# Reordering the vector work between two matmul stages: Sinkhorn rounds, token sums, a maximum and a scaling

## The chip, the cores and the metric

One core of a Trainium2 chip runs the whole program. The metric is device time in microseconds (us) of that core, from one launch; smaller is better. TensorE (PE in the profile, PEld for its weight loads) does the matrix products, VectorE (DVE) and ScalarE (ACT) do elementwise work, GpSimd (POOL) does elementwise work on SBUF, and SyncE (SP) issues the DMAs.

## What is computed

Three stages follow each other. The middle of the reference, cut:

```python
attn_out = _attn_ref(**attn_kwargs)             # bucketed attention, 2 x 8 heads, 768 x 64
x = attn_out.transpose(0, 2, 1, 3).reshape(1536, 512)
h = x @ w_in                                    # 512 -> 2048
x = (h * np.tanh(softplus(h))) @ w_out          # 2048 -> 512
# mixture of 8 experts, every token through every expert
logits = x @ w_gate
P = np.exp(logits - logits.max())
for _ in range(8):
    P /= P.sum(1, keepdims=True) + 1e-09        # rows: over 8 experts
    P /= P.sum(0, keepdims=True) + 1e-09        # columns: over 1536 tokens
    P *= N / E
for e in range(8):
    out += P[:, e:e + 1] * (np.maximum(x @ w1[e], 0.0) @ w2[e])
```

The eight rounds of rows and columns (Sinkhorn rounds) work on a matrix of 1536 tokens by 8 experts. It is held as `prob`, 128 partitions x 12 x 8.

## The kernel before, in words

Every float32 product is made of three matmuls on rounded parts: high by high, high by low, low by high. The low part of a matrix is the difference between it and its rounded copy. For weights ScalarE writes the high part and GpSimd the low part; for activations VectorE writes the low part.

**Attention** takes the first part of the time and is not touched.

**The MLP** runs 48 steps (`steps`, L818). A step `n` issues 12 matmuls of `up` (L831 to L833) into a PSUM bank; ScalarE applies Mish and rounds (`act`, L841, L842), and VectorE writes the rest `gl` (L843). `down(n - 3)` then adds 12 matmuls (L856) into four banks. When a group of four steps ends for a block of 512 tokens, VectorE adds the four banks into `acc` (`evacuate`, L866). Every engine executes its instructions in the order in which they were issued. A side table (`at`) issues further work at the end of a step: the gate logits of a token block (`logits`: eight matmuls at L884, transposes at L890, an addition at L891), and the sums and differences of activations that the next stage needs (`make_t`, L987 to L998). For each of two chunks `kc` there are four sums, k = 1, 2, 4, 3. Numbers 1 and 3 take four VectorE instructions, numbers 2 and 4 three; the last of them waits for a ScalarE copy.

**The expert stage** runs 64 units, each a quarter of one expert for half of the tokens. A unit's first part is seven products `s` = 0 to 6 of six matmuls (L1141), into two PSUM banks; after each, `post` lets ScalarE and VectorE read the bank. After product 1, VectorE makes the total `u` from its bank (L1161), and product 3 adds to that same bank, so it waits for this read. After product 6 VectorE writes four rests `gl` (L1154). Then 36 matmuls of `second` (L1208) follow in four runs, 0 to 3. A table of jobs (`job(u, s, ...)`) hangs further work behind product `s` of unit `u`, or, with s = 7 to 10 (`NP1` is 7), behind the runs of `second`. The slot (u, 8) carries the next weights' splitting (`unit_a_hi`, `unit_s_hi` on ScalarE; `unit_a_lo` at L1010, L1011 and `unit_s_lo` at L1027 on GpSimd) and, in units 1 to 8, one Sinkhorn round on VectorE. The job (u, -1) splits the next `w` matrix (ScalarE L1030, GpSimd L1034). Every fourth unit VectorE also takes finished output tiles out of PSUM (`gather`, L1220 to L1226).

A round is `sinkhorn_rows` (reduce L920, add L921, reciprocal L922, product L923) and `sinkhorn_cols` (reduce L926, transposes L902, reduce L903, add L928, reciprocal L929, transposes L932, product L933), each instruction on the result of the one before.

Of the kernel before, what the change touches and what calls it, by code (L numbers as in the profile page):

```python
# [12 lines left out]
AF = mybir.ActivationFunctionType  # L13
ALU = mybir.AluOpType
AX = mybir.AxisListType

P = 128
# [36 lines left out]
Q = 32  # L54
# [7 lines left out]
def lsh_attention_moe_kernel(  # L62
# [13 lines left out]
    nc = tc.nc  # L76
# [727 lines left out]
    prob = acc_p.tile([P, NTOK // P, E], F32, name="prob")  # L804
# [88 lines left out]
    def small(name, p, n=1):  # L893
        return sk_p[0].tile([p, n], F32, tag=name, name=name)

    def quarters(x):
        return [x[a * Q:(a + 1) * Q] for a in range(P // Q)]

    def across(x, op, negate=False):
        y, r = small("y", Q, P), small("r", Q)  # L900
        for a, part in enumerate(quarters(x)):
            nc.vector.transpose(out=y[:, a * Q:(a + 1) * Q], in_=part)  # L902
        nc.vector.tensor_reduce(out=r, in_=y, axis=AX.X, op=op, negate=negate)  # L903
        return r

    def sinkhorn_max():
        m = small("m", P)
        nc.vector.tensor_reduce(out=m, in_=prob, axis=AX.XY, op=ALU.max)
        r = across(m.to_broadcast([P, Q]), ALU.max, negate=True)
        m = small("nm", P)  # L910
        for part in quarters(m):
            nc.vector.tensor_copy(part, r)
        return m

    def sinkhorn_exp(r):
        nc.scalar.activation(prob, prob, AF.Exp, bias=r[:, 0:1])
# [20 lines left out]
    def tile_of(i):  # L937
        return acc[:, i // KC, i % KC, :]

    def scale_first(i):  # L940
        dst = tile_of(i)
        nc.vector.tensor_scalar(out=dst, in0=dst, scalar1=prob[:, i, 0:1], scalar2=None, op0=ALU.mult)
        nc.vector.scalar_tensor_tensor(
            out=dst, in0=tile_of(i + NT // 2), scalar=prob[:, i, 1:2], in1=dst, op0=ALU.mult, op1=ALU.add
        )
# [4 lines left out]
    def at(n, f, *args):  # L950
        side.setdefault(n, []).append(lambda: f(*args))

    box = {}

    def put(key, f, *keys):
        def g():
            box[key] = f(*[box[k] for k in keys])
        return g

    LAG = 3  # L960
    done_at = {tb: n + LAG for n, (g, tb, _) in enumerate(steps) if g == NG - 1}
    for tb in range(NTB - 1):
        at(done_at[tb] + (6 if tb else 3), logits, tb)

    tw = []

# [78 lines left out]
        parts_t(0, k, kc, a)  # L1045
        held[kc] = a

    for n, k, kc in ((1, 1, 0), (2, 2, 0), (2, 4, 0), (3, 3, 0), (3, 1, 1), (4, 2, 1), (4, 4, 1), (5, 3, 1)):
        at(done_at[1] + n, make_t, k, kc)
    free = {}  # L1050
    for n, (_, _, i) in enumerate(steps):
# [182 lines left out]
    def job(u, s, f, *args):  # L1234
        jobs.setdefault((u, s), []).append(lambda: f(*args))

    NP1 = len(PRODUCTS)
# [13 lines left out]
    for f in splits:  # L1251
        job(0, 5, f)
    job(0, NP1 + 2, logits, NTB - 1, ps_u, "u0")
    job(1, 0, put("m", sinkhorn_max))
    job(1, 2, lambda: sinkhorn_exp(box["m"]))
    for x in range(8):
        job(1 + x, NP1 + 1, sinkhorn_rows)
        job(1 + x, NP1 + 1, sinkhorn_cols)
    for i in range(NT // 2):
        job(9 + i // 3, NP1 + 1, scale_first, i)  # L1260

    half = NU // 2

# [95 lines left out]
```

## Time and profile before

| what | value |
|---|---|
| median of three runs | 1553.04 us (1551.37 to 1553.8) |
| the profiled execution's own time | 1551.87 us |
| its span, first to last instruction | 1550.0 us |
| TensorE busy, of the span | 98%, weight loads 87% |
| VectorE, ScalarE, GpSimd busy | 61%, 45%, 61% |
| share of the chain of waits by engine | PE 83%, DVE 11% |

A busy TensorE row is no measure of its speed, since matmuls overlap. What a stage costs is read from the length of a unit, and what it lost from the idle time in front of TensorE's instructions and weight loads.

### The profile page before, as it was taken

The numbers are of one execution on the slowest core, as the hardware profiler recorded it, in microseconds if no ns is written. First come the engines' busy times: TensorE is split into PE (matmuls) and PEld (weight loads), VectorE is DVE, ScalarE is ACT, GpSimd is POOL, SyncE is SP. The second block draws the span as 40 slices with busy tenths as digits, with TensorE's granted clock in tenths as the row PEclk, the third lists the DMA queues.
The fourth block names the chain that finished last, engine by engine and source line by source line (L and its number), as shares of the span: only waits on it lengthen the run. The fifth ranks groups of instructions, "written<-read, shape, count | busy, mean of one in ns | idle before, by whom it ended". The sixth has DMA issues, their size and how long they took to land.

```text
span 1550.0 us, 20648 instructions
## 1 busy us (share of the span) xinstructions
PE 1523.0 (98%) x7492; PEld 1348.1 (87%) x7492; DVE 945.6 (61%) x1546; ACT 694.1 (45%) x1266; POOL 941.2 (61%) x785
## 2 busy tenths in 40 slices
PE   8999999999999999999999999999999999999999
PEld 7898888888888887888989898999999999999998
DVE  8899995867633678787453557654535344445353
ACT  5878776654423343333333334343333333333331
POOL 6888876433313485656666666667666666666661
PEclk9999999999999999999999999999999999999999
DMA  7755540222200122121222222223222222222211
GB/s 188 164 141 139 150 118 15 82 68 82 69 27 1 41 69 69 57 66 58 70 65 70 67 69 67 69 67 110 68 69 68 69 68 69 68 69 68 69 55 41
DMA packets 65989, 117.67 MB, mean 76 GB/s; under 512 B 18320, under 2 KB 19320, under 8 KB 65888
## 3 DMA queue, kind: packets, MB, share of 16 engines
q1 hardware_dynamic: 65888, 116.36, 25.6%
q8 instruction: 59, 0.97, 0.3%
q14 instruction: 42, 0.34, 0.1%
HBM read 93.41 MB, written 3.15 MB: 62 GB/s over the span
## 4 chain that ended last, share of the span: by engine, by line
PE 83%; DVE 11%; issue 2%; POOL 1%; ACT 1%; DMA 1%; SPq 0%; DVEq 0%; ACTq 0%; POOLq 0%
PE y L1208 30%; PE u L1141 29%; PE y L856 7%; PE pav L488 4%; PE h L833 2%; PE h L832 2%; PE h L831 2%; DVE gl L1154 1%; PE pst L438 1%; PE pst L439 1%; PE ps L386 1%; DVE mx L400 1%; DVE prob L923 1%; POOL plo L450 0%; DMA vt<-in_v_dram 0%
## 5 line engine op out<-in xcount | busy, mean ns | idle before, releaser
L1149 ACT ACTIVATE gh<-c 128x384 fp32r<-128x384 f32 x256 | 134.7, 526 | 192.5 <-DVE c L1161 190.4
L1154 DVE SCALAR_TENSOR_TENSOR gl<-c,gh 128x384 fp32r<-128x384 f32 x256 | 195.5, 827 | 0.0
L1161 DVE TENSOR_TENSOR u<-u,p 128x384 f32<-128x384 f32 x64 | 35.6, 556 | 258.2 <-PE u L1141 258.2
L1208 PE MATMUL y<-ww,gh 128*128 128x512 f32 x768 | 186.6, 391 | 0.0
L1208 PE MATMUL y<-w,gh 128*128 128x512 f32 x768 | 186.0, 391 | 0.0
L1208 PEld LDWEIGHTS y<-w,gh 128*128 128x128 f32 x768 | 143.7, 188 | 28.9
L1208 PEld LDWEIGHTS y<-ww,gh 128*128 128x128 f32 x768 | 143.7, 188 | 28.8
L450 POOL TENSOR_TENSOR plo<-p,ph 128x384 fp32r<-128x384 f32 x128 | 139.9, 1105 | 30.3 <-ACT ph L447 16.8
L1034 POOL TENSOR_TENSOR w<-stage,w 128x1024 fp32r<-128x1024 f32 x32 | 76.6, 2393 | 92.0 <-ACT w L1030 92.0
L1034 POOL TENSOR_TENSOR ww<-stage,ww 128x1024 fp32r<-128x1024 f32 x32 | 76.6, 2392 | 84.2 <-ACT ww L1030 84.2
L856 PE MATMUL y<-gh,w 128*128 128x512 f32 x336 | 109.9, 389 | 0.0
L444 ACT ACTIVATE p<-pst 128x384 f32<-128x384 f32 x192 | 92.5, 486 | 38.0 <-PE pst L439 32.2
L1030 ACT CAST ww<-stage 128x1024 fp32r<-128x1024 f32 x32 | 33.6, 1049 | 162.3 <-PE y L1208 162.3
L1030 ACT CAST w<-stage 128x1024 fp32r<-128x1024 f32 x32 | 33.6, 1049 | 161.3 <-PE y L1208 161.3
L1141 PE MATMUL u<-tw,w 128*128 128x384 f32 x480 | 94.2, 342 | 9.5 <-DVE u L1161 9.5
L1010 POOL TENSOR_TENSOR wx<-stage,wx 128x512 fp32r<-128x512 f32 x32 | 44.9, 1403 | 96.1 <-ACT wx L1005 91.2
L148 POOL TENSOR_TENSOR stage<-stage,sgn 128x512 f32<-128x512 f32 x32 | 43.0, 1345 | 99.1 <-DVE sgn L146 93.6
L400 DVE TENSOR_REDUCE mx<-ps 128x1 f32<-128x768 f32 x95 | 90.0, 948 | 15.1 <-PE ps L386 14.3
L1010 POOL TENSOR_TENSOR wa<-stage,wa 128x512 fp32r<-128x512 f32 x32 | 45.6, 1424 | 87.8 <-ACT wa L1005 87.8
L1208 PE MATMUL y<-ww,gl 128*128 128x512 f32 x384 | 98.2, 389 | 0.0
L1208 PE MATMUL y<-w,gl 128*128 128x512 f32 x384 | 97.4, 389 | 0.0
L1141 PE MATMUL u<-tw,ws 128*128 128x384 f32 x480 | 92.1, 337 | 4.2 <-DVE u L1161 4.1
(232 smaller groups left out, 3996.6 us busy)
## 6 DMA issues: line engine op xcount, KB each, us to landing
stage<-in_w_dram SPq DMA_DIRECT2D x160, 512.0 KB
raw<-in_qk_dram SPq DMA_DIRECT2D x13, 384.0 KB
wx<-hi SPq DMA_DIRECT2D x20, 192.0 KB
vt<-in_v_dram SPq DMA_DIRECT2D x16, 192.0 KB
out_dram<-acc SPq DMA_DIRECT2D x11, 256.0 KB
zq<-hi SPq DMA_DIRECT2D x11, 192.0 KB
ak<-hi SPq DMA_DIRECT2D x11, 192.0 KB
zq<-lo SPq DMA_DIRECT2D x11, 192.0 KB
```

What stands on the lines that cost most here:

```text
L400: nc.vector.tensor_reduce(out=m[:, t, 0:1], in_=s_t[t][:, :, :HALF], axis=AX.XY, op=ALU.max, negate=True)
L444: nc.scalar.activation(p_t[u, c], st_t.pop((u, c))[:, :HALF], AF.Exp, scale=0.125)
L450: (nc.gpsimd if e == "P" else nc.vector).tensor_sub(out, in0, in1)
L488: nc.tensor.matmul(av_t[u][:, :HALF], x.rearrange("p a d -> p (a d)"), y, start=False, stop=(c == NKC - 1 and n == len(pairs) - 1),)
L856: nc.tensor.matmul(yps[j], x, y, start=(head and m == 0), stop=(tail and m == 2))
L1010: nc.gpsimd.tensor_sub(a[:, 1, 0:512], t[:, 0, :], f32(a)[:, 0, 0:512])
L1030: nc.scalar.copy(wbuf[u % 2]["w"][:, 0, :], staged["u", u, 1].rearrange("p c n -> p (c n)"))
L1034: nc.gpsimd.tensor_sub(y[:, 1, :], t, f32(y)[:, 0, :])
L1141: nc.tensor.matmul(bank[x], weight(u, a, m, kc), moving(u, b, mm, kc), start=(first and n == 0), stop=(n == 5), skip_group_check=not first)
L1149: nc.scalar.activation(hi, src, AF.Relu)
L1154: nc.vector.scalar_tensor_tensor(out=lo, in0=src, scalar=0.0, in1=f32(hid_u[u, c][0]), op0=ALU.max, op1=ALU.subtract)
L1208: nc.tensor.matmul(y_t[t], (hi, hi, lo)[m][:, t % 3 * P:(t % 3 + 1) * P], y, start=(k == 0 and first), stop=(k == NF // 2 - 1 and last),)
```

## The change

```diff
     def sinkhorn_max():
         m = small("m", P)
         nc.vector.tensor_reduce(out=m, in_=prob, axis=AX.XY, op=ALU.max)
-        r = across(m.to_broadcast([P, Q]), ALU.max, negate=True)
+        return across(m.to_broadcast([P, Q]), ALU.max, negate=True)
+
+    def sinkhorn_spread(r):
         m = small("nm", P)
...
     def scale_first(i):
         dst = tile_of(i)
-        nc.vector.tensor_scalar(out=dst, in0=dst, scalar1=prob[:, i, 0:1], scalar2=None, op0=ALU.mult)
+        nc.scalar.activation(dst, dst, AF.Copy, scale=prob[:, i, 0:1])
...
-        at(done_at[tb] + (6 if tb else 3), logits, tb)
+        at(done_at[tb] + 3, logits, tb)
...
-    for n, k, kc in ((1, 1, 0), (2, 2, 0), (2, 4, 0), (3, 3, 0), (3, 1, 1), (4, 2, 1), (4, 4, 1), (5, 3, 1)):
+    for n, k, kc in ((1, 1, 0), (1, 2, 0), (2, 4, 0), (2, 3, 0), (3, 1, 1), (3, 2, 1), (4, 4, 1), (4, 3, 1)):
         at(done_at[1] + n, make_t, k, kc)
...
-    job(1, 0, put("m", sinkhorn_max))
-    job(1, 2, lambda: sinkhorn_exp(box["m"]))
+    job(1, 1, put("r", sinkhorn_max))
+    job(1, 3, put("m", sinkhorn_spread, "r"))
+    job(1, NP1, lambda: sinkhorn_exp(box["m"]))
     for x in range(8):
         job(1 + x, NP1 + 1, sinkhorn_rows)
-        job(1 + x, NP1 + 1, sinkhorn_cols)
+        job(2 + x, NP1 + 1, sinkhorn_cols)
     for i in range(NT // 2):
-        job(9 + i // 3, NP1 + 1, scale_first, i)
+        job(10 + i // 3, NP1 + 1, scale_first, i)
```

`done_at[1]` is step 42. The sums of steps 43 to 47 now stand in steps 43 to 46, two in each, and the logits of the second token block are issued in step 45 instead of step 48. Unit 1 does the rows of the first round alone, units 2 to 8 the columns of a round and the rows of the next, and unit 9 the last columns. The scaling of the first tiles follows in units 10 and 11.

**VectorE in the slot of a Sinkhorn round.** Before, the first rows behind a unit's rests, up to the total of the next unit:

```order
L920 TENSOR_REDUCE rsum<-prob 128x12
L921 TENSOR_SCALAR rsum<-rsum 128x12
L922 RECIPROCAL rsum<-rsum 128x12
L923 TENSOR_TENSOR prob<-prob,rsum 128x96
L926 TENSOR_REDUCE csum<-prob 128x8
L902 STREAM_TRANSPOSE y<-csum 32x32 x4
L903 TENSOR_REDUCE r<-y 32x1
L928 TENSOR_SCALAR r<-r 32x1
L929 RECIPROCAL r<-r 32x1
L932 STREAM_TRANSPOSE i<-r 32x32 x4
L933 SCALAR_TENSOR_TENSOR prob<-i,prob 128x96
L1161 TENSOR_TENSOR u<-u,p_6284 128x384
```

The same slot of units 2 to 8 now (the lines behind the edit are two higher):

```order
L928 TENSOR_REDUCE csum<-prob 128x8
L902 STREAM_TRANSPOSE y<-csum 32x32 x4
L903 TENSOR_REDUCE r<-y 32x1
L930 TENSOR_SCALAR r<-r 32x1
L931 RECIPROCAL r<-r 32x1
L934 STREAM_TRANSPOSE i<-r 32x32 x4
L935 SCALAR_TENSOR_TENSOR prob<-i,prob 128x96
L922 TENSOR_REDUCE rsum<-prob 128x12
L923 TENSOR_SCALAR rsum<-rsum 128x12
L924 RECIPROCAL rsum<-rsum 128x12
L925 TENSOR_TENSOR prob<-prob,rsum 128x96
L1163 TENSOR_TENSOR u<-u,p_6268 128x384
```

The same eleven rows stand in front of the total, with the seven of the columns ahead of the four of the rows.

**VectorE at the end of the MLP.** Before, from the rest of step 46 (`t` and `tw` are the sums of the next stage, `lgs` the logits):

```order
L843 TENSOR_TENSOR gl<-t,gh 128x512
L992 TENSOR_TENSOR t<-xh,xl 128x384
L993 TENSOR_TENSOR t<-t 128x384
L998 TENSOR_TENSOR tw<-t,tw 128x384
L992 TENSOR_TENSOR t<-xh,xl 128x384
L993 TENSOR_TENSOR t<-t 128x384
L998 TENSOR_TENSOR tw<-t,tw 128x384
L843 TENSOR_TENSOR gl<-t,gh 128x512
L987 TENSOR_TENSOR t<-xh 128x384
L988 TENSOR_TENSOR t<-xl 128x384
L989 TENSOR_TENSOR t<-t 128x384
L998 TENSOR_TENSOR tw<-t,tw 128x384
```

Now, from the same rest:

```order
L843 TENSOR_TENSOR gl<-t,gh 128x512
L994 TENSOR_TENSOR t<-xh,xl 128x384
L995 TENSOR_TENSOR t<-t 128x384
L1000 TENSOR_TENSOR tw<-t,tw 128x384
L989 TENSOR_TENSOR t<-xh 128x384
L990 TENSOR_TENSOR t<-xl 128x384
L991 TENSOR_TENSOR t<-t 128x384
L1000 TENSOR_TENSOR tw<-t,tw 128x384
L843 TENSOR_TENSOR gl<-t,gh 128x512
L866 TENSOR_TENSOR acc<-y_5711,acc 128x512
L866 TENSOR_TENSOR acc<-y_5715,acc 128x512
L866 TENSOR_TENSOR acc<-y_5719,acc 128x512
```

The last sum of four instructions stood behind the rest of step 47 (the second `gl`) and stands ahead of it now; the logits' transposes, which followed that sum, have moved up behind the rest of step 45.

## Rows read from the trace of the kernel before

**Rows 1.** Waits of TensorE's weight loads from 255 us on: total, times, longest us

```profile
PEld u L1141 <- DVE u L1161: 16.9, 10, 3.1
```

**Rows 2.** Stretches of units 0, 1, 3, 4, 8, 10: busy time by engine, PEclk, DMA

```profile
530.41:551.43 21.02, 19.22 (x88) 16.45 (x87) 13.96 (x24) 9.71 (x18) 16.77 (x14) 0.92 0.09 25
551.43:567.35 15.92, 15.78 (x79) 14.02 (x78) 12.63 (x27) 7.54 (x12) 13.90 (x11) 1.00 0.44 133
...
584.19:601.02 16.83, 15.80 (x80) 14.04 (x78) 13.53 (x27) 5.88 (x10) 9.97 (x8) 1.00 0.20 63
601.02:619.65 18.63, 15.81 (x80) 14.04 (x79) 16.89 (x33) 5.88 (x10) 9.94 (x8) 1.00 0.18 58
...
670.15:690.36 20.21, 17.39 (x80) 15.63 (x78) 17.02 (x33) 5.88 (x10) 9.94 (x8) 0.92 0.17 53
...
707.18:722.72 15.54, 15.54 (x80) 14.09 (x78) 11.70 (x16) 5.89 (x10) 10.28 (x8) 1.00 0.23 69
```

**Rows 3.** VectorE in order of time, units 1 and 2: start, us, line, idle before

```profile
553.62 0.62 DVE L912 COPY nm<-r 32x1 f32<-32x1 f32 x4
...
579.63 0.24 DVE L920 TENSOR_REDUCE rsum<-prob 128x12 f32<-128x96 f32 x1
579.91 0.43 DVE L921 TENSOR_SCALAR rsum<-rsum 128x12 f32<-128x12 f32 x1
...
580.63 2.13 DVE L923 TENSOR_TENSOR prob<-prob,rsum 128x96 f32<-128x96 f32 x1
582.80 0.33 DVE L926 TENSOR_REDUCE csum<-prob 128x8 f32<-128x96 f32 x1
...
584.35 0.14 DVE L928 TENSOR_SCALAR r<-r 32x1 f32<-32x1 f32 x1
...
585.60 2.40 DVE L933 SCALAR_TENSOR_TENSOR prob<-i,prob 128x96 f32<-128x96 f32 x1
587.92 0.55 DVE L1161 TENSOR_TENSOR u<-u,p 128x384 f32<-128x384 f32 x1
```

**Rows 4.** GpSimd in order of time, the same units

```profile
552.72 2.38 POOL L1027 TENSOR_TENSOR w<-sraw,w 128x1024 fp32r<-128x1024 f32 x1
...
579.26 1.05 POOL L1011 TENSOR_TENSOR wx<-stage,wx 128x256 fp32r<-128x256 f32 x1
580.27 2.39 POOL L1027 TENSOR_TENSOR w<-sraw,w 128x1024 fp32r<-128x1024 f32 x1
585.51 2.38 POOL L1034 TENSOR_TENSOR w<-stage,w 128x1024 fp32r<-128x1024 f32 x1 [2.86 <-ACT w L1030]
```

**Rows 5.** VectorE in order of time, the end of the MLP and unit 0

```profile
509.51 1.84 DVE L843 TENSOR_TENSOR gl<-t,gh 128x512 fp32r<-128x512 f32 x1 [1.54 <-ACT gh L842]
...
516.60 2.48 DVE L866 TENSOR_TENSOR acc<-y,acc 128x512 f32<-128x512 f32 x4
...
520.00 0.55 DVE L992 TENSOR_TENSOR t<-xh,xl 128x384 f32<-128x384 f32 x1
...
522.20 0.55 DVE L992 TENSOR_TENSOR t<-xh,xl 128x384 f32<-128x384 f32 x1
...
525.90 1.12 DVE L843 TENSOR_TENSOR gl<-t,gh 128x512 fp32r<-128x512 f32 x1 [1.42 <-ACT gh L842]
...
531.11 1.26 DVE L890 STREAM_TRANSPOSE lgs<-lg 32x128 f32<-32x128 f32 x4
...
534.91 0.55 DVE L1161 TENSOR_TENSOR u<-u,p 128x384 f32<-128x384 f32 x1
```

**Rows 6.** TensorE in order of time, the end of the MLP and unit 0

```profile
527.91 0.39 PE L856 MATMUL y<-gl,w 128*128 128x512 f32 x1
...
535.51 2.94 PE L1141 MATMUL u<-tw,w 128*128 128x384 f32 x12 [1.80 <-DVE u L1161]
```

**Rows 7.** Instructions on the tile `acc`: count, then ns minimum/median/maximum, first and last start

```profile
L942 DVE TENSOR_SCALAR acc<-acc,prob x6: 474/480/954, 702.6 to 723.0; 128x512 f32<-128x512 f32 x6
```

**Rows 8.** The page's costliest groups: ScalarE's copy of a 128x1024 matrix

```profile
L1030 ACT CAST ww<-stage 128x1024 fp32r<-128x1024 f32 x32 | 33.6, 1049 | 162.3 <-PE y L1208 162.3
```

## The prediction, made before the result was known

> **What bounds the kernel now.** TensorE does, and it is rarely idle. I first read the waits of its weight loads from 255 us on, because after the attention nearly all time is a chain of matmuls. One kind of wait is left that matters: products of a unit held up by VectorE's total `u`, ten times, 16.9 us in all, at most 3.1 us [rows 1]. So the change can win about that much and what hangs on it, and no more.
>
> Next I cut the time at the first product of each unit [rows 2]. Unit 10 takes 15.54 us and shows a granted clock of 1.00, and later units are within 0.03 us of it: this is a unit without a wait. Units 2, 3, 5, 6, 7 and 9 take 16.82 to 16.84 us (unit 3's row stands for the six), units 4 and 8 take 18.63 and 20.21, unit 1 takes 15.92, and unit 0 takes 21.02. In units 0 and 8 the granted clock averages 0.92. At full speed for the rest, that is some 3.4 us at the lower level (1.2 instead of 2.4 GHz), worth 1.6 us: the clock fell after the long wait. In unit 4, whose wait was as long, it did not fall. So the losses to take back are 6 x 1.29 = 7.7, 3.09 and 4.67 in units 2 to 9, together 15.5, then 0.4 in unit 1. Unit 0 holds the logits of the last block besides, so I take its loss from its wait, 1.80 [rows 6], and 1.6 for the clock: 3.4.
>
> Why is `u` late? In the slot behind unit 2, VectorE runs one round from 579.63 to 588.00, and then `u` starts at 587.92 [rows 3]. The small product L923 takes 2.13 us and the small product L933 takes 2.40, although nothing in their size asks for it. The GpSimd rows explain it [rows 4]: L923 ends 0.11 us after the 1024-wide subtraction that began at 580.27 (580.27 + 2.39 = 582.66), and L933 ends 0.11 us after the next one (585.51 + 2.38 = 587.89). VectorE's instruction waited for GpSimd's to finish, and L933 lost the race to the splitting of the next `w` by 0.09 us (585.51 against 585.60). The unit behind lost 1.29 us [rows 2], so the latest harmless end of the chain is 588.00 - 1.29 = 586.7.
>
> **The change part by part.**
>
> *Columns before rows.* The slot starts at the same point of a unit, 579.63 in unit 2's times, since the rests ahead of it are unchanged. The column half now comes first. From its first reduction to its product it took 582.80 to 585.60, or 2.80 us, free of GpSimd. So the product comes to 582.43, waits for the subtraction that ends at 582.66, and is done at 582.8. The row half needs 1.00 us from its start to its product (579.63 to 580.63, some of it a wait), and that product some 0.3 when it isn't held. The chain ends near 584.1, before the splitting of the next `w` starts at 585.51, and 2.6 us before it would hurt. Both long waits are gone because the held instruction now falls in the pause between the two subtractions, 2.86 us long by GpSimd's row [rows 4]. The gathers of units 4 and 8 follow an earlier chain too, so their whole loss goes.
>
> One step of this is not shown by the trace of before: the one-column addition L928 took 0.14 us while GpSimd was idle [rows 3], and now it meets the subtraction, 1.55 us into the chain, at 581.2. Below: it isn't held, as the four one-column copies at 553.62 weren't (0.62 us for four, while L1027 ran from 552.72 to 555.10 [rows 3, 4]). Above: it is held to 582.66 and the chain comes 1.5 us later, with its last product starting at 585.0 to 585.3, just ahead of 585.51. I take the lower, the nearest row. Either way the waits go.
>
> The Trainium skill (SBUF — State Buffer, section Who interferes with whom) says that VectorE's copies and scalar operations may take the port pair shared with GpSimd and are then blocked for the whole of a GpSimd instruction. By that rule the addition would be held, and the sum would be the same with 0.2 to 0.5 us to spare in place of 1.4. The four copies disagree with it for one column, so I keep it as a danger and not as the forecast.
>
> *Fewer rounds per slot at the ends.* Unit 1 has rows alone, so unit 2 has no wait; unit 9 has columns alone. Gain: units 2 to 9 all return to 15.54, 15.5 us.
>
> *The maximum behind the total.* In unit 1 the chain up to the copies stood in front of `u`. Now the reduction and transposes stand between `u` and `v`, and the copies between `v` and the next total, where two products' time covers them. Gain 0.4. The exponential moves behind product 6 on ScalarE, and delays the weight copies behind it, for which nothing waits in that unit (rows alone, and GpSimd's work is for a unit later).
>
> *Scaling on ScalarE.* VectorE loses six instructions of 0.48 us [rows 7]. ScalarE gains six: above, 1.05 us each, the price of a copy twice as wide, and below, nothing. ScalarE waits 162 us in all for TensorE at that line alone [rows 8], so three a unit are covered; units 10 and 11 had no wait before either. Zero, at worst 0.4 us in unit 11, where the gathers follow.
>
> *Token sums and logits.* Here the change can cost. VectorE's queue before: the rest of step 45 ends at 511.35 (509.51 + 1.84), two sums of four instructions follow up to 516.60, so 2.65 each; a sum of three takes 2.20 (520.00 to 522.20); the bank additions and the rest of step 46 take 3.40 (516.60 to 520.00); from the last sum's start to the rest of step 47 it is 3.70 (522.20 to 525.90), and that rest takes 1.12 [rows 5]. Now a sum of four stands ahead of the rest of step 45. It fills that rest's 1.54 us of waiting, so the rest ends between 1.1 and 2.65 later; I take 2.0, because ScalarE's copies move with it: 513.3. Logits' transposes 1.3: 514.6. Sums 2.65 and 2.20: 519.5. Bank additions and rest: 522.9. Sum of three: 525.1. Sum of four up to the rest of step 47, 3.70 + 0.45: 529.3. The rest ends at 530.4. TensorE reads it at 527.91 [rows 6], and the logits moved ahead don't alter that time. So the last `down` waits 2.5 us; bounds 1.6 and 3.2, or 0 if VectorE's short waits inside the sums fill up. In return unit 0 starts with a shorter queue: the sum and the transposes at 531.11 are gone from in front of `u`, which then waits for its product alone, and 3.4 us come back. What is late next is that last `down` in place of product 3. Net 0.9.
>
> **Sum.** 15.5 + 0.4 + 0.9 = 16.8 us off the profiled execution's 1551.87, which gives 1535.1. It lay 1.2 under the median, so the median goes to 1553.04 - 16.8 = 1536.2.
>
> **The rivals.**
>
> *The clock falls at the new wait.* The last `down` waits 2.5 us. Of the three waits of 1.8 us or more, two were followed by the lower clock, at 1.6 us each [rows 2]. For it: the wait is new and of that size. Against: it comes in two short pieces, for the rounded part and then for its rest. 1536.2 + 1.6 = 1537.8.
>
> *No wait at the last down.* The queue closes up, no 2.5 us are lost: 1533.7.
>
> *The waits stay: the change doesn't do what it reorders for.* If the column half is held longer than I bound it, by 1.5 us and 0.3 more, the last row product meets the subtraction that starts at 585.51 and ends at 588.00, as L933 does now. Seven slots keep their wait; gone are one of 1.29, 0.4 and 0.9, which is 2.6: 1550.4. For it stands the thin margin of the held case, against it the one-column copies.
>
> *Slower: two waits in the row half.* Should the column half end after 585 (5.4 us instead of 3.2), the scalar addition of the rows meets the subtraction from 585.51, ends at 588.0, and the row product 0.3 us behind it meets GpSimd's next instruction, which lasts up to 1.05 by the row of a 256-wide one [rows 4]. The chain would end about 1 us later than now in seven slots: 7 x 1.05 = 7.4, less 2.6, so 1557.8. It takes 2.2 us of delay in a half that runs alone, and only one instruction there is in doubt, worth 1.5.
>
> **How the numbers follow.** Forecast 0.45, clock 0.2, no wait 0.15; a mixture in which a few slots keep their wait, 1540 to 1546, 0.08; waits stay 0.08; slower 0.04. A difference of 0.2% (3.1 us) is about what a measurement of this kernel can tell from no change. Faster: 0.45 + 0.2 + 0.15 + 0.08 = 0.88; same 0.08; slower 0.04. The range holds the first three: from 1533.7, less 1.2 for the spread of the runs, 1532.5, up to 1537.8 with the upper bound of the new wait (0.7), 0.4 in unit 11 and the spread: 1540. That leaves out 0.2.
>
> **What would show it.** Units 2 to 9 at 15.54 us each; the column product ending close behind the GpSimd subtraction, and the row product under 0.4 us; no wait for L1163's `u` over 0.3 us. A wait of 1.6 to 3.2 us at L856 for the rest of step 47, which ends near 530.4, and unit 0 some 3.4 us shorter. I am wrong if the row product in a slot still takes 2 us, or if the last `down` loses more than 3.2 us.

## The result, and the profile after

The changed kernel takes 1538.18 us (median of six runs, 1536.14 to 1542.4), the kernel before in the same session 1552.69 (six runs, 1551.37 to 1554.56). The ratio is 0.9909, with a 95% interval of 0.9892 to 0.9927. The forecast was 1536.2 with a range of 1532.5 to 1540.0: the time lies in the range, 2.0 us above the point. The profiled execution took 1536.53 us.

The page of the changed kernel, busy time by engine and the chain by engine:

```profile
PE 1518.2 (99%) x7492; PEld 1344.9 (88%) x7492; DVE 907.7 (59%) x1540; ACT 698.4 (46%) x1272; POOL 940.9 (61%) x785
...
PE 87%; DVE 7%; POOL 2%; issue 1%; DMA 1%; ACT 1%; SPq 0%; DVEq 0%; POOLq 0%; ACTq 0%
```

VectorE's share of the chain fell from 11% to 7%, and GpSimd's share of the span hardly moved. No work went away. What changed is who stands in whose way, and the waits of TensorE's weight loads from 255 us on say that best (total, times, longest):

```profile
PEld lg L884 <- POOL xl L872: 2.5, 3, 1.1
PEld y L856 <- ACT w L1025: 1.0, 1, 1.0
PEld y L856 <- DVE gl L843: 1.0, 1, 1.0
PEld y L856 <- ACT gh L842: 0.9, 1, 0.9
PEld h L833 <- POOL w L168: 0.5, 1, 0.5
```

The ten waits for `u`, 16.9 us in all [rows 1], are gone. In their place stand three waits at L856. Two are at the last `down`, for ScalarE's rounded part `gh` and its rest `gl`, as the prediction expected. The third, whose weight load is put down to L1025, lies three steps earlier, where the matmul itself waits for the bank additions of step 43; the prediction did not have it. Nor did it have the waits of the logits (L884) for GpSimd's low parts. The wait at L833 is older than the change.

The stretches of units 0, 1, 2, 4 and 8, cut as in [rows 2]:

```profile
533.03:552.36 19.33, 17.77 (x87) 14.86 (x86) 9.49 (x16) 9.53 (x17) 15.87 (x14) 1.00 0.10 28
552.36:567.88 15.52, 15.52 (x79) 14.07 (x78) 9.38 (x24) 7.55 (x12) 14.46 (x11) 1.00 0.44 126
567.88:583.40 15.52, 15.52 (x80) 14.07 (x79) 9.44 (x26) 5.89 (x10) 10.00 (x8) 1.00 0.25 79
...
598.91:614.45 15.54, 15.54 (x80) 14.10 (x78) 12.48 (x32) 5.88 (x10) 9.97 (x8) 1.00 0.22 69
...
661.07:676.61 15.54, 15.54 (x80) 14.10 (x78) 12.48 (x32) 5.88 (x10) 9.99 (x8) 1.00 0.22 68
```

In each unit shown after unit 0 the length equals TensorE's busy time in it, and no unit from 1 to 9 takes more than 15.54 us: nothing is waited for, the gathers of units 4 and 8 included. The clock shows 1.00 everywhere. Units 2 to 9 took 139.8 us before (567.35 to 707.18) and take 124.3 now (567.88 to 692.15). Unit 0 is the exception. It is 1.69 us shorter than before, not 3.4, and 19.33 - 17.77 = 1.56 us of it are idle.

VectorE in the slot behind unit 2 (start, us, line, idle before; compare [rows 3]):

```profile
578.84 0.32 DVE L928 TENSOR_REDUCE csum<-prob 128x8 f32<-128x96 f32 x1
...
580.38 0.14 DVE L930 TENSOR_SCALAR r<-r 32x1 f32<-32x1 f32 x1
...
581.63 0.35 DVE L935 SCALAR_TENSOR_TENSOR prob<-i,prob 128x96 f32<-128x96 f32 x1
...
582.30 0.17 DVE L923 TENSOR_SCALAR rsum<-rsum 128x12 f32<-128x12 f32 x1
...
582.77 0.26 DVE L925 TENSOR_TENSOR prob<-prob,rsum 128x96 f32<-128x96 f32 x1
...
585.77 0.56 DVE L1163 TENSOR_TENSOR u<-u,p 128x384 f32<-128x384 f32 x1 [2.74 <-PE u L1143]
```

GpSimd at the same time (compare [rows 4]):

```profile
579.47 2.39 POOL L1029 TENSOR_TENSOR w<-sraw,w 128x1024 fp32r<-128x1024 f32 x1
584.72 2.40 POOL L1036 TENSOR_TENSOR w<-stage,w 128x1024 fp32r<-128x1024 f32 x1 [2.86 <-ACT w L1032]
```

Read the two together. The column product L935 ends at 581.98, 0.12 us after GpSimd's subtraction (579.47 + 2.39 = 581.86). The row product follows inside GpSimd's pause and takes 0.26 us where it took 2.13. The chain is over at 583.03, 1.7 us before the next subtraction. The total `u` starts at 585.77 after 2.74 us of waiting for its product: VectorE now waits for TensorE, not the other way round.

### The profile page after: what moved, and what is told of

It is laid out like the page before. It is cut to its first block, busy times and chain, and to the rows that moved or that the text cites. A ratio compares the mean times of both kernels' runs of the same rounds, so it can differ in the third digit from the quotient of the medians.

```text
span 1534.7 us, 20649 instructions
## 1 busy us (share of the span) xinstructions
PE 1518.2 (99%) x7492; PEld 1344.9 (88%) x7492; DVE 907.7 (59%) x1540; ACT 698.4 (46%) x1272; POOL 940.9 (61%) x785
## 4 chain that ended last, share of the span: by engine, by line
PE 87%; DVE 7%; POOL 2%; issue 1%; DMA 1%; ACT 1%; SPq 0%; DVEq 0%; POOLq 0%; ACTq 0%
PE y L1210 34%; PE u L1143 30%; PE y L856 7%; PE pav L488 3%; PE h L833 2%; PE h L831 2%; PE h L832 2%; DVE mx L400 2%; PE pst L438 1%; PE pst L439 1%; PE ps L386 1%; POOL plo L450 1%; DVE vs L355 0%; DMA vt<-in_v_dram 0%; DMA sq<-row 0%
## 5 line engine op out<-in xcount | busy, mean ns | idle before, releaser
L856 PE MATMUL y<-gh,w 128*128 128x512 f32 x336 | 110.2, 390 | 1.2 <-DVE acc L866 0.6
```

The lines of the kernel that those rows point to most:

```text
L856: nc.tensor.matmul(yps[j], x, y, start=(head and m == 0), stop=(tail and m == 2))
```

## The experiments

Each edit is made in the kernel before or in the changed one, as said. Its ratio is to the kernel before in its own session (1552.17 to 1552.94 us). One thing about the attention, which no edit touches, must be known first. The first held matmul of the MLP shows where the attention ended. In the changed kernel (TensorE, in order of time):

```profile
273.94 0.50 PE L833 MATMUL h<-xh,w 128*128 128x512 f32 x1
```

and in the run with both later edits together, told of below:

```profile
276.54 0.50 PE L833 MATMUL h<-xh,w 128*128 128x512 f32 x1
```

That is 2.6 us between two executions in work that is the same, so edits worth 1 or 2 us are told apart by the lengths of stages, and the medians stand beside them. I call "end of unit 1" the time from that matmul to the first product of unit 2. It is 293.4 us before and 293.95 in the changed kernel.

### The order of rows and columns by itself (kernel before)

```diff
-        job(1 + x, NP1 + 1, sinkhorn_cols)
+        job(2 + x, NP1 + 1, sinkhorn_cols)
-        job(9 + i // 3, NP1 + 1, scale_first, i)
+        job(10 + i // 3, NP1 + 1, scale_first, i)
```

> The kernel before with the columns moved one unit later, and the scaling with them, and nothing else. Theory (VectorE's small products were held by GpSimd's subtractions, and the new order puts the held one into GpSimd's pause): units 2 to 9 take 15.54 us each in the profile, the columns' product about 0.35 us, the rows' product under 0.5 us; units 0 and 1 stay at 21.0 and 15.9; the time falls by 15.5 us or 1.0%, to about 1537. Rival (the gain needs the token sums or the maximum to be moved too): units 3 to 9 stay at 16.8 or more, and the time falls by 1.3 to 3 us only.

Measured: 1537.69 us (four runs, 1536.68 to 1539.24), ratio 0.9906 (0.9891 to 0.992). Units 2 and 12 of its profile:

```profile
568.23:583.77 15.54, 15.54 (x80) 14.10 (x78) 9.44 (x26) 5.89 (x10) 9.98 (x8) 1.00 0.23 69
...
723.47:740.02 16.55, 15.79 (x80) 14.02 (x79) 10.98 (x18) 5.89 (x10) 10.08 (x8) 1.00 0.21 64
```

Units 2 to 9 all take 15.51 to 15.54, and units 0 and 1 are as before (21.01 and 15.92). So the new place of the columns gives the whole of the 15.5 us without the other moves. Unit 12 brought a surprise: a new wait that makes it 1.0 us longer. With it the account is 15.5 - 1.0 = 14.5, and the medians differ by 14.6.

### The chain as it was, GpSimd's next subtraction later (kernel before)

```diff
-        job(u, -1 if u else NP1, unit_w_hi, u + 1)
-        job(u, -1 if u else NP1, unit_w_lo, u + 1)
+        job(u, 2 if u else NP1, unit_w_hi, u + 1)
+        job(u, 2 if u else NP1, unit_w_lo, u + 1)
```

> The kernel before, with rows and columns in their old order, and only the splitting of the next w matrix moved from the start of a unit to behind product 2, on ScalarE and GpSimd both. Theory (the columns' product waits for that subtraction and for nothing else): the product at L933 falls from 2.40 us to under 0.8, no total waits for it, units 2 to 9 return to 15.54 and the time falls by 15 us as with the new order; the rows' product at L923 still takes 2.1. Rival (the round is simply too long for the slot, or the order of its instructions is what matters): units 2 to 9 stay at 16.8, no change beyond 2 us.

Measured: 1540.52 us (four runs), ratio 0.9924 (0.991 to 0.9939). VectorE in the slot of unit 2:

```profile
579.74 2.13 DVE L923 TENSOR_TENSOR prob<-prob,rsum 128x96 f32<-128x96 f32 x1
...
584.70 0.26 DVE L933 SCALAR_TENSOR_TENSOR prob<-i,prob 128x96 f32<-128x96 f32 x1
```

and the two 1024-wide subtractions on GpSimd:

```profile
579.37 2.39 POOL L1027 TENSOR_TENSOR w<-sraw,w 128x1024 fp32r<-128x1024 f32 x1
...
588.70 2.40 POOL L1034 TENSOR_TENSOR w<-stage,w 128x1024 fp32r<-128x1024 f32 x1 [3.92 <-ACT w L1030]
```

The order on VectorE is the old one. L923, which still meets the subtraction ahead of it, still takes 2.13 us and ends 0.11 us after it. L933, which no longer meets one, takes 0.26 instead of 2.40. This shows the reason by itself: the small instruction is long only because GpSimd is at work. Of the 15 us expected, 11.8 came. The chain still ends later, 17.6 us after the start of unit 2 (584.96 - 567.38) against 15.15 with the change, and small waits for `u` are left: units 4 and 8 take 16.48 and unit 2 15.91, so units 2 to 9 take 126.5 us, 13.3 less than before. And units 10 and 11, which had no wait before, take 16.27 each: there the scaling (L942) now meets the moved work of GpSimd, and behind each of units 9 and 10 takes about 0.95 us three times, where two of the three had taken 0.48.

### Token sums and logits put back (changed kernel)

```diff
-        at(done_at[tb] + 3, logits, tb)
+        at(done_at[tb] + (6 if tb else 3), logits, tb)
-    for n, k, kc in ((1, 1, 0), (1, 2, 0), (2, 4, 0), (2, 3, 0), (3, 1, 1), (3, 2, 1), (4, 4, 1), (4, 3, 1)):
+    for n, k, kc in ((1, 1, 0), (2, 2, 0), (2, 4, 0), (3, 3, 0), (3, 1, 1), (4, 2, 1), (4, 4, 1), (5, 3, 1)):
```

> The changed kernel with the token sums and the logits of the second block put back where they were. Theory (the two-per-step sums cost 2.6 us at the last down and hand back less, because the last logits then wait for GpSimd): unit 0 starts at 530.4 instead of 533.0 us, the wait for the total in unit 0 is back at 1.8 us, units 2 to 9 stay at 15.5; against the changed kernel the profile is shorter by 1 us where the clock doesn't fall and longer by 0.6 where it does. Rival (the sums' move is a gain of its own): 1 to 3.5 us slower than the changed kernel.

Measured: 1536.47 us (four runs, 1535.44 to 1537.74), ratio 0.9897 (0.988 to 0.9913). Units 0 and 1:

```profile
531.47:552.52 21.05, 19.25 (x88) 16.47 (x86) 13.94 (x24) 9.71 (x18) 16.67 (x14) 0.92 0.09 25
552.52:568.06 15.54, 15.54 (x79) 14.10 (x78) 9.33 (x24) 7.54 (x12) 13.56 (x11) 1.00 0.40 126
```

Unit 0 has its wait for `u` and its lower clock back, and no wait is left at the last `down` or at the logits. The end of unit 1 is at 292.98 against 293.95 with the change: this part of the change costs about 1 us, where the prediction had it gain 0.9. The expectation had this kernel 0.6 us longer wherever the clock falls in unit 0; it fell, and the stages are 1 us shorter all the same. Unit 1 against that of the first experiment (15.92) gives the price of the maximum in two parts: 0.4, as forecast. Without the token part the account is 15.5 + 0.4 = 15.9, and the medians differ by 15.8.

### Scaling on VectorE, maximum in one piece (changed kernel)

```diff
-        nc.scalar.activation(dst, dst, AF.Copy, scale=prob[:, i, 0:1])
+        nc.vector.tensor_scalar(out=dst, in0=dst, scalar1=prob[:, i, 0:1], scalar2=None, op0=ALU.mult)
...
-    job(1, 1, put("r", sinkhorn_max))
-    job(1, 3, put("m", sinkhorn_spread, "r"))
-    job(1, NP1, lambda: sinkhorn_exp(box["m"]))
+    job(1, 0, put("r", sinkhorn_max))
+    job(1, 0, put("m", sinkhorn_spread, "r"))
+    job(1, 2, lambda: sinkhorn_exp(box["m"]))
```

> The changed kernel with the scaling back on VectorE and the maximum, its spreading and the exponential back in front of the totals of unit 1. Theory: the scaling is worth nothing (units 10 and 11 at 15.54 either way), and the maximum 0.4 us at most, in unit 1; in all 0 to 0.5 us slower than the changed kernel. Rival (ScalarE's scaling is what keeps units 10 and 11 clean): one of them at 16 us or more.

Measured: 1538.96 us (four runs), ratio 0.9912 (0.9897 to 0.9927). VectorE behind unit 11, where the gathers (L1228) follow the scaling:

```profile
719.98 2.77 DVE L945 SCALAR_TENSOR_TENSOR acc<-acc,prob 128x512 f32<-128x512 f32 x1
...
725.03 2.06 DVE L1228 SCALAR_TENSOR_TENSOR acc<-y,prob,acc 128x512 f32<-128x512 f32 x3
727.00 0.55 DVE L1163 TENSOR_TENSOR u<-u,p 128x384 f32<-128x384 f32 x1
```

Here `u` is late again and unit 12 takes 16.54 us, the same 1.0 us as in the first experiment, which the expectation (0 to 0.5 us) had not seen. Some 2 us of the slot are the old hold again: L945 takes 2.77 us beside GpSimd's subtraction, where the two after it take 0.75 each. In the changed kernel unit 12 takes 15.51. So scaling on ScalarE is what lets the scaling move one unit on; in the units where it stood before it cost nothing on VectorE. The maximum in front of `u` cost nothing here: unit 1 takes 15.51. It is worth its 0.4 only beside the old token sums.

### GpSimd's sums for unit 2 behind the low parts (changed kernel)

GpSimd around the last block's low parts, in the changed kernel:

```profile
540.92 0.74 POOL L1019 TENSOR_TENSOR sraw<-stage 128x256 f32<-128x256 f32 x1
541.73 0.94 POOL L1020 TENSOR_TENSOR sraw<-sraw,stage 128x256 f32<-128x256 f32 x1
542.64 1.05 POOL L1021 TENSOR_TENSOR sraw<-stage 128x256 f32<-128x256 f32 x1
543.65 1.05 POOL L1022 TENSOR_TENSOR sraw<-stage,sraw 128x256 f32<-128x256 f32 x1
544.66 5.32 POOL L872 TENSOR_TENSOR xl<-acc,xh 128x512 fp32r<-128x512 f32 x4
```

and TensorE's logits there:

```profile
548.81 0.42 PE L884 MATMUL lg<-xl,wgr 128*32 128x512 f32 x1 [0.75 <-POOL xl L872]
550.03 0.42 PE L884 MATMUL lg<-xl,wgr 128*32 128x512 f32 x1 [0.81 <-POOL xl L872]
```

The two waits are the 1.56 us that unit 0 idles. Four sums for weights that are needed much later stand in front of `xl`, 3.8 us in all; in the kernel before they took 2.9, and here VectorE's rests run beside them from 541.01 on. The edit lets them follow it:

```diff
-            job(u, 0 if u else 4, unit_s, u + 2)
+            job(u, 0 if u else 6, unit_s, u + 2)
```

> The changed kernel with one job moved: in unit 0 GpSimd makes the sums of unit 2's weights (L1019 to L1022) behind product 6 instead of product 4, so behind the low parts of the last token block. Theory (the last logits wait for these low parts, which stood behind the sums): the two waits of 0.8 us at L884 in unit 0 go, unit 0 falls from 19.33 to about 17.4 us, the rest stays; 1.9 us faster than the changed kernel. Rival (the low parts are late because ScalarE's copies are): the waits stay, no change.

Measured: 1536.77 us (four runs), ratio 0.9893 (0.988 to 0.9907). Units 0 and 1:

```profile
534.52:551.93 17.41, 17.41 (x87) 14.96 (x86) 10.60 (x16) 8.62 (x17) 13.65 (x13) 1.00 0.11 32
551.93:567.87 15.94, 15.84 (x80) 14.07 (x79) 10.26 (x23) 8.43 (x13) 15.86 (x12) 1.00 0.33 100
```

Unit 0 falls to 17.41 and has no idle time. This confirms GpSimd's queue as the cause of the missing 1.7 us. What was late next is in unit 1, a wait of 0.4 us for a copy on ScalarE, which now stands behind the high part of those same sums. Together 1.5 us are won by stages (end of unit 1 at 292.4).

### The last sum behind the rest of step 47 (changed kernel)

```diff
-... (4, 4, 1), (4, 3, 1)):
+... (4, 4, 1), (5, 3, 1)):
```

> The changed kernel with only the last token sum (number 3 of the second chunk, four instructions) put back into step 47, behind that step's rest. Theory (that sum is what makes the last rest late): the waits of the last down for the rounded part and its rest, 0.5 and 0.6 us with their weight loads 0.9 and 1.0, go; the wait of 0.65 us for the banks of step 43 stays; unit 0 starts at 531.1 instead of 533.0; no wait for the total in unit 0 above 0.3; about 2 us faster, and a steadier time, since the clock doesn't fall. Rival (the logits' transposes are to blame): unit 0 still starts after 532.5.

Measured: 1536.32 us (four runs, 1534.68 to 1540.37), ratio 0.9895 (0.9877 to 0.9912). Of the three waits at L856 the two in the last `down` are gone, and the one for the bank additions stays (0.68 us of TensorE's time). The MLP, up to the first product of unit 0, is 1.7 us shorter, unit 0 unchanged at 19.35, and the end of unit 1 is at 292.3. That the times would be steadier was not met: one run showed a granted clock of 0.998 and 1540.37 us.

### Both edits together (changed kernel)

> Both edits together, on the changed kernel: the last token sum back in step 47, and GpSimd's sums of unit 2's weights behind product 6 in unit 0. Theory: the gains add, 2 and 1.9 us, so unit 0 starts at 531.1 and takes 17.4, the profile 3.9 us under the changed kernel's, and the spread of the runs shrinks because no wait over 1 us is left in front of TensorE. Rival (one uncovers the other): 2 us or less.

Measured: 1537.09 us (five runs, 1536.06 to 1538.22), ratio 0.9897 (0.9884 to 0.9911). By stages the two nearly add up: the end of unit 1 is at 291.1, or 2.8 us under the change, where the two alone gave 1.5 and 1.7. Unit 0 takes 17.88 us, 0.5 more than with the GpSimd edit alone, and holds a short wait for `u` again (0.2 us on TensorE, 0.5 on a weight load). The profiled execution was expected 3.9 us under that of the changed kernel and took 1536.62 us against 1536.53: its attention was the 2.6 us longer one shown above. The median is only 1.1 us under the change.

### Two more moves, and the change once more

Beside the two edits, the second sum of chunk 1 goes back to its own step, and ScalarE's and GpSimd's splitting of unit 2's sums leaves the end of unit 0 for the start of unit 1:

```diff
-... (3, 1, 1), (3, 2, 1), (4, 4, 1), (5, 3, 1)):
+... (3, 1, 1), (4, 2, 1), (4, 4, 1), (5, 3, 1)):
...
-            job(u, NP1 + 1, unit_s_hi, u + 2)
+            job(u if u else 1, NP1 + 1 if u else 0, unit_s_hi, u + 2)
...
-            job(u, NP1 + 1, unit_s_lo, u + 2)
+            job(u if u else 1, NP1 + 1 if u else 0, unit_s_lo, u + 2)
```

> The kernel with both edits and two more: the token sum number 2 of the second chunk back in step 46, so that the bank additions of step 43 no longer wait behind it, and the high and low parts of unit 2's weight sums (L1025, L1029) moved from the end of unit 0 to behind product 0 of unit 1, so that ScalarE's copy of product 0 is not held up by them. Theory: the bank wait of 0.7 us at L856 and the 0.4 us wait of unit 1 both go, unit 1 falls from 15.93 to 15.54, and the time from the MLP's first held matmul to the end of unit 1 falls by 0.9 us against both edits, 3.7 us against the changed kernel. Rival (VectorE's queue is full, so the last rest is late again): a wait of 0.5 us or more returns at the last down, and nothing is won.

The changed kernel in the same session:

> The changed kernel once more, on the same chip as the four edits and with the same runs of before. Theory: units 2 to 9 at 15.5, unit 0 near 19.3 without and near 21 with a fall of the clock; the single times fall into groups about 1.6 to 3 us apart by how often the clock fell after the waits at the end of the MLP; median 1536 to 1540, and 3 to 4 us above the four edits. Rival (the spread is the attention's): the groups show no tie to the granted clock, and the four edits' gain is lost in it.

Measured: 1535.51 us with the four edits (five runs, 1534.45 to 1537.95; ratio 0.9892, 0.9878 to 0.9905) and 1538.51 with the change as it was (six runs, 1536.57 to 1540.08; ratio 0.9909, 0.9895 to 0.9922). The medians are 3.0 us apart, the stages 3.2 (end of unit 1 at 290.7 and 293.9), where 3.7 had been expected; against both edits 0.4 came of the 0.9. The intervals of the two ratios overlap, so the stages carry that difference. Units 0 and 1 with the four edits:

```profile
532.65:551.41 18.76, 17.69 (x88) 14.91 (x86) 12.90 (x20) 9.07 (x17) 14.43 (x13) 1.00 0.10 29
551.41:566.95 15.54, 15.54 (x79) 14.10 (x78) 10.68 (x23) 8.60 (x13) 15.38 (x12) 1.00 0.35 102
```

and the waits of its weight loads from 255 us on:

```profile
PEld u L1143 <- DVE u L1163: 1.4, 1, 1.4
PEld h L833 <- POOL w L168: 0.5, 1, 0.5
```

No wait but the old one at L833 is left in the MLP, and none in unit 1. One of 1.07 us on TensorE (18.76 - 17.69) is left in unit 0. VectorE reaches `u` no later than in the run with only the last sum put back (260.2 and 260.3 us behind the first held matmul). TensorE comes 1.0 us sooner, since the wait for the banks is gone, and now waits for `u`. By its median and by its stages this is the fastest version run.

That the executions of the change fall in two groups by clock was met only in part. In the first session the three with a clock of 1.0 took 1536.14 to 1536.92 us, and the three at 0.997 to 0.999 took 1539.43 to 1542.4. In the second session executions with a clock of 1.0 took 1536.57 to 1539.4. The time goes with the clock in the first session; in the second 2.8 us of spread stand beside an unchanged clock. The length of the attention is another source of spread, seen between profiles; what sets it stays open.

## Why the prediction was right, and where it was off

| term of the sum | predicted, us | measured by stages, us |
|---|---|---|
| units 2 to 9 | -15.5 | -15.6 (139.8 to 124.3) |
| unit 1 | -0.4 | -0.4 (15.92 to 15.52) |
| last `down` | +2.5 | +2.6 (unit 0 starts at 533.03, not 530.41) |
| unit 0 | -3.4 | -1.7 (21.02 to 19.33) |
| scaling on ScalarE | 0 | 0 (units 11 and 12 without a wait) |
| sum | -16.8 | -15.1; profiled executions 1551.87 - 1536.53 = 15.3 |

**Columns before rows: right, cause and size.** That VectorE's products are held by GpSimd was read in the trace of before from ends that lay 0.11 us apart, and the second experiment, which moves GpSimd and leaves VectorE's order alone, shows it. One step was a little off without consequence. I let the slot start at the old point of the unit, 12.3 us in (579.63 - 567.35). It starts 11.0 us in (578.84 - 567.88), since the 1.29 us that unit 2 lost before lay ahead of it. The chain then takes 4.19 us (578.84 to 583.03) against the 4.5 forecast.

**The one-column addition: the lower bound was right.** All eight in the changed kernel (count, then ns minimum, median, maximum):

```profile
L930 DVE TENSOR_SCALAR r<-r x8: 141/142/142, 580.4 to 689.1; 32x1 f32<-32x1 f32 x8
```

The one in unit 2's slot starts at 580.38, in the middle of GpSimd's subtraction, and takes no longer than when GpSimd was idle [rows 3]. The Trainium skill (SBUF — State Buffer, section Who interferes with whom) says that a scalar operation can enter a mode that takes the shared ports and then blocks, when its operands meet certain conditions. The danger that the prediction drew from it did not come true for this operation of one column, and the measurement decides.

A wider scalar operation is held. This is the addition to the twelve row sums in unit 1's slot of the kernel before:

```profile
564.03 2.08 DVE L921 TENSOR_SCALAR rsum<-rsum 128x12 f32<-128x12 f32 x1
```

and GpSimd at that time:

```profile
563.38 2.70 POOL L1027 TENSOR_TENSOR ws<-sraw,ws 128x1024 fp32r<-128x1024 f32 x1
```

The addition ends at 566.11, 0.03 us after the subtraction. In GpSimd's pause the same addition takes 0.17 us (L923 in the changed kernel, shown above). So one column was not held in any of the eight slots, and twelve columns were; where between them the limit lies, no run here tests.

For products with two inputs from SBUF the same section of the Trainium skill says that they contend with GpSimd's reads, and here the trace agrees: 2.13 and 2.40 us became 0.26 and 0.35.

**Token sums at the last `down`: right in time, one wait more than foreseen.** VectorE at the end of the MLP (compare [rows 5]):

```profile
511.42 1.84 DVE L843 TENSOR_TENSOR gl<-t,gh 128x512 fp32r<-128x512 f32 x1 [1.54 <-ACT gh L842]
...
521.85 1.09 DVE L843 TENSOR_TENSOR gl<-t,gh 128x512 fp32r<-128x512 f32 x1
...
529.23 1.11 DVE L843 TENSOR_TENSOR gl<-t,gh 128x512 fp32r<-128x512 f32 x1 [1.42 <-ACT gh L842]
...
535.40 0.56 DVE L1163 TENSOR_TENSOR u<-u,p 128x384 f32<-128x384 f32 x1 [1.48 <-PE u L1143]
```

The rests of steps 45, 46 and 47 end at 513.26, 522.94 and 530.34, where the prediction had 513.3, 522.9 and 530.4. TensorE pays for it three times:

```profile
520.29 0.47 PE L856 MATMUL y<-gh,w 128*128 128x512 f32 x1 [0.65 <-DVE acc L866]
...
529.25 0.50 PE L856 MATMUL y<-gh,w 128*128 128x512 f32 x1 [0.52 <-ACT gh L842]
...
530.40 0.50 PE L856 MATMUL y<-gl,w 128*128 128x512 f32 x1 [0.65 <-DVE gl L843]
```

It reads the rest at 530.40, 2.49 us later than before, as forecast. But the prediction looked for this loss at the last `down` alone, as one wait of 1.6 to 3.2 us for the rest, and that wait itself is 0.65. The first of the three waits, for the banks of step 43, was not in it, and the runs price it: with only the last sum put back the MLP is 1.7 us shorter, and the other 0.9 come back in the run with four edits, where the wait for the banks goes too.

**Unit 0: here the prediction failed.** It said that `u` then waits for its product alone, "and 3.4 us come back", and named the last `down` as what is late next. The first half holds: the last VectorE row above shows `u` waiting 1.48 us for TensorE, and the clock stays at 1.00. But a second thing was late next. In the old, longer unit 0 the last block's low parts were in time. This is GpSimd in the kernel before:

```profile
542.11 6.35 POOL L872 TENSOR_TENSOR xl<-acc,xh 128x512 fp32r<-128x512 f32 x4 [0.92 <-DVE c L1161]
```

It began on them 11.7 us into unit 0 then (542.11 - 530.41) and does so 11.6 us in now (544.66 - 533.03). With `u` no longer late, TensorE comes to them 3.6 us sooner (14.4 us into the unit instead of 18.0) and waits 1.56 us. So the token part is 2.6 - 1.7 = 0.9 of loss where the sum had 0.9 of gain. Those 1.8 us, less 0.1 won in units 2 to 9, are the miss of the sum by stages (-15.1 for -16.8). The profiled execution missed by 1.4 us (1536.53 for 1535.1) and the median by 2.0, and the rest of these is spread between executions. The experiment that lets `xl` go ahead of the four sums brings unit 0 to 17.41, close to the 17.6 (21.02 - 3.4) that the prediction implied. I had looked at VectorE's queue alone. The question I left out was whether GpSimd, busy for most of unit 0, could follow when the unit became shorter.

**Scaling on ScalarE: zero was right, the reason incomplete.** The prediction compared it with the scaling where it stood before, where VectorE had room. The same edit moves the scaling one unit on, and there it would have cost 1.0 us on VectorE, as two runs show. On ScalarE a scaling takes 0.71 us, inside the bounds, and no unit waits for it. The 0.4 us of unit 1 came as forecast, but not by the maximum alone: the moved token sums give them too, as the run with the maximum in one piece shows (15.51).

**The rivals.** That the clock falls at the new waits did not happen in the profiled execution. In the first session, though, three of six runs showed a mean clock of 0.997 to 0.999, and the median of six lies between the two groups. This rival had been given 0.2 and 1537.8 us, and may be part of why the median lies further from the point than the profile does. That the queue closes up and nothing is lost at the last `down` is excluded by the two waits there. That the waits stay, or that the rows take two of them, is excluded by the slot: 0.35 and 0.26 us for the two products, in a pause with 1.7 us to spare, and at most 0.35 and 0.49 over all eight slots.

## What to carry to other kernels

When a tiny instruction takes microseconds, look at what the neighbouring engine is doing until just before it ends; here, moving two such instructions out of its way cost nothing and brought 2.13 and 2.40 us down to 0.26 and 0.35. When a wait is removed, list every input that the shortened stretch consumes, on all engines, since the wait was also their cover. And judge edits of 1 or 2 us by the lengths of the stages that they touch, not by the median of a few whole runs.

## What was not expected of the hardware

The attention, which no edit touches, ended up to 3.2 us apart between profiled executions (first held matmul of the MLP at 273.3 to 276.5 us). TensorE's waits for a DMA there differ between them as well, from none to 3.0 us, but the longest wait was not in the longest attention. The spread is more than any single one of the later edits is worth.

A wait on TensorE does not always bring the lower clock. In the kernel before two of its three waits of 1.8 us or more did [rows 2], and in the first three experiments unit 0, which keeps its wait of 1.8 us, shows 0.92 each time. In the changed kernel, whose waits after the attention hold TensorE for less than 1 us each, the profile shows no fall.

The mean clock of a whole execution has to be read with care. In the run with both edits it is 0.999, yet the clock stands at 1.00 up to 1532 us, and averages 0.70 only in the last 2.7 us, behind the last matmul, where it costs nothing. By an estimate from these two numbers that end takes 0.0005 off the mean. So a mean of 0.999 in another run need not be a fall that costs time, while 0.997 and 0.998 speak for one further ahead; where it lies in the changed kernel, no profile here shows.
